# Attention and feed-forward on one core: the written-out order of the first 677 steps is replaced by another order of the same steps

## The chip, the core and the metric

The kernel runs on one core of a Trainium2 chip. The metric is the device time of one execution in microseconds (us). The instructions of the program are spread over five queues: TensorE (PE in the profile, its weight loads PEld), VectorE (DVE), ScalarE (ACT), GpSimd (POOL) and SyncE (SP, which issues most of the DMAs). Each queue runs its instructions in the order in which the program writes them, and waits on semaphores where one needs the result of another.

## What is computed

```python
scale = 1.0 / np.sqrt(q.shape[-1])                       # q, k, v: 8 x 12 x 448 x 64
scores = scale * np.matmul(q, k.transpose(0, 1, 3, 2)) - np.log(S)
attn = 1.0 / (1.0 + np.exp(-scores))                     # a sigmoid, no softmax
x = np.matmul(attn, v)                                   # to 3584 tokens x 768
h = x @ w_in                                             # 768 x 2048
g = np.where(h > 0.0, h, np.exp(np.minimum(h, 0.0)) - 1.0)
out = g @ w_out                                          # 2048 x 768
```

The eight batches have 448 tokens each. Both weights arrive as 64-bit floats. The kernel splits every operand of the feed-forward part into a high and a low fp16 part and adds three products.

## The kernel before

The work goes batch by batch: attention on pairs of heads, then the first layer (`moe1...`, x times w_in, 16 feature blocks f of 128), then the second layer (`moe2`, g times w_out). All queues are filled by hand (`manual_schedule`), so the order in which Python calls the steps is the order on every engine.

For the first part of the program that order is a table, `ORDER` (line 25), a text of 677 tokens. `first_stage` (line 1403) goes through it and calls one function for each token. A token's instructions go to the end of their engines' queues at that moment. So a token can only be moved against others of the same engine; across engines the semaphores decide. The table covers the attention of batches 0 and 1, the preparation of both weights, the first and second layer of batch 0, and ends where the first layer of batch 1 starts ("the second first layer": `next(h)` behind `first_stage`, line 1500). The tokens:

- `q k v i n` with a number load a pair's rows on SP. `T` turns queries and keys on TensorE, `Y` copies them, `Sn.t` makes scores, `Gn.t` is the sigmoid on ScalarE, `Vn.t` multiplies by the values on TensorE, `H` and `I` write the result's two parts, `M Q N` measure the values.
- `l A b B C D d E F` load and split one of eight units of w_in (`w_in_parts`, line 280). The 64-bit words lie in the tile `stage`.
- `x0` to `x15` are the products of batch 0's first layer, 18 matmuls each (`moe1_products`, line 890). `y` (ScalarE, line 907), `j` (VectorE), `z` (ScalarE, line 1390) and `w` (VectorE, line 1393) turn block f into g.
- `o0` to `o18` load w_out in 19 pieces (`w_out_parts`, line 436). For each piece, `a` (ScalarE, line 222) and `e` (ScalarE, line 230) take the words apart, `c` (VectorE, line 235) joins them, `g` adds their sizes on TensorE (line 244, tile `so`), `s` (VectorE, line 251) puts the sign back. When all pieces of a half have gone through `g`, `m0` or `m1` (`w_out_scale`, line 497) makes that half's scale, and only then `h` (ScalarE, line 475) and `p` (VectorE, line 481) write the fp16 parts. Pieces 0 to 7 are the first half, 8 to 18 the second.
- `X0` to `X95` are steps of three matmuls of batch 0's second layer (line 1115), sixteen to an output tile. X0 to X47 need the first half of w_out, X48 to X95 the second. `O0` to `O5` scale and store a tile.
- `K` is one piece of `make_sums` (line 422): VectorE and ScalarE write sums of blocks of w_in into the tile `room`, and the next `K` has GpSimd store them (line 420). `room` has three places for results. Later batches load these sums.

The raw words of a two-row piece of w_out are staged in the half of the tile `wo` that is not yet needed:

```python
SLOTS = 0, 4, 8, 12, 0, 4, 8, 12, 8, 12, 8, 12, 12      # by piece
w = wo[:, 1, SLOTS[k] : SLOTS[k] + 4]
```

So the load of piece 9 waits for `s7`, that of piece 11 for `s9`, that of piece 12 for `s11`: they share the place 12. Pieces 13 to 15 have a tile each, pieces 16 to 18 reuse them, so `o16` waits for `s13`.

Of the kernel before, what the change touches and what calls it, by code (L numbers as in the profile page):

```python
# [22 lines left out]

UNITS = 0, 4, 8
ORDER = """
n0 q0 q1 v0 i0 k0 k1 v1 l0 i1 T0 T1 Y0 q2 M0 Y1 S0.0 q3 S0.1 G0.0 l1 G0.1 Q0 S1.3 N0 v2
V0.0 G1.3 S0.2 b0 v3 S1.0 v13 V0.1 G0.2 k2 G1.0 S1.1 V0.2 A0 k3 V1.0 S1.2 G1.1 B0 G1.2
V1.1 C0 b1 l2 V1.2 D0 v12 V1.3 A1 M1 v4 T2 v5 H1 n1 H0 T3 I1 Y2 Q1 q5 I0 Y3 S2.0 S2.1
G2.0 N1 G2.1 S2.2 B1 V2.0 G2.2 q4 S3.3 d0 b2 S3.0 V2.1 G3.3 M2 l3 V2.2 E0 S3.1 k5 C1
G3.0 F0 Q2 k4 G3.1 S3.2 N2 V3.0 A2 V3.1 R0 G3.2 B2 b3 V3.2 V3.3 D1 T4 H2 d1 H3 T5 q6 Y4  # L30
C2 v7 I2 Y5 S4.0 l4 E1 S4.1 v6 I3 q7 R1 G4.0 k6 F1 G4.1 S5.3 V4.0 G5.3 D2 S4.2 A3 S5.0
d2 V4.1 G4.2 B3 l5 E2 S5.1 k7 V4.2 G5.0 M3 C3 G5.1 S5.2 V5.0 b4 D3 V5.1 F2 Q3 G5.2 T6 q8
Y6 V5.2 N3 A4 V5.3 d3 T7 H4 S6.0 q9 Y7 I4 v8 E3 S7.3 v9 B4 l6 G6.0 k8 F3 C4 G7.3 k9 S6.1
H5 V6.0 D4 G6.1 S6.2 I5 b5 V6.1 R2 S7.0 G6.2 d4 Rq G7.0 V6.2 S7.1 A5 Rr0 l7 S7.2 V7.0
G7.1 B5 G7.2 V7.1 T8 M4 V7.2 q10 C5 Y8 V7.3 b6 T9 Q4 S8.0 q11 H7 d5 H6 k10 Y9 D5 E4 I6
G8.0 S8.1 F4 v11 I7 v10 G8.1 V8.0 k11 S8.2 A6 N4 V8.1 G8.2 S9.0 B6 E5 V8.2 S9.1 M5 G9.0
C6 G9.1 S9.2 V9.0 b7 F5 V9.1 Q5 G9.2 T10 N5 q12 Y10 V9.2 d6 A7 S9.3 S10.0 D6 G9.3 B7
G10.0 S10.1 k12 V9.3 G10.1 r1 T11 H9 S10.2 H8 o13 I9 Y11 q13 C7 I8 G10.2 S11.3 r2 V10.0
V10.1 d7 D7 e13 S11.0 G11.3 k13 E6 V10.2 G11.0 F6 S11.1 S11.2 G11.1 V11.0 o14 G11.2 Wn
V11.1 E7 P12 V11.2 V11.3 x0 H10 o15 e14 H11 F7 I10 o0 x1 y0 Rr1 I11 e15 x2 y1 e0 o1 j1  # L40
a0 j0 z1 x3 c0 y2 z0 j2 w0 e1 o2 w1 z2 g0 x4 y3 s0 a1 w2 c1 j3 e2 o3 g1 x5 s1 y4 z3 j4
a2 w3 z4 c2 x6 y5 w4 o4 e3 j5 a3 z5 c3 g2 y6 w5 x7 s2 e4 o5 j6 a4 z6 c4 g3 x8 y7 w6 s3
j7 e5 o6 a5 g4 x9 s4 z7 y8 w7 c5 j8 a6 o7 g5 x10 s5 e6 y9 c6 z8 j9 w8 g6 z9 x11 s6 e7 w9
a7 o8 y10 c7 j10 g7 y11 x12 s7 z10 m0 e8 o9 w10 a8 x13 j11 h0 c8 y12 z11 p0 w11 e9 g8
x14 s8 a9 j12 o10 h1 c9 y13 z12 p1 g9 y14 x15 s9 h2 w12 p2 e10 o11 j13 a10 h3 c10 X0 X1
y15 p3 g10 z13 X2 s10 X3 h4 X4 j15 X5 e11 X6 a11 X7 p4 z15 c11 X8 h5 X9 w13 g11 s11 p5
o12 j14 X10 h6 X11 p6 z14 w14 X12 h7 X13 w15 p7 e12 X14 K a12 X15 X16 c12 X17 X18 O0 g12
X19 s12 X20 X21 a13 X22 a14 c13 X23 a15 X24 K c14 g13 c15 X25 s13 g14 g15 X26 s15 o16
X27 s14 o17 o18 X28 X29 X30 X31 X32 O1 X33 a16 X34 K e16 X35 X36 c16 X37 g16 X38 s16 X39
X40 e17 X41 a17 X42 K X43 c17 X44 g17 X45 s17 X46 X47 a18 O2 e18 c18 g18 m1 s18 h8 p8  # L50
X48 h9 X49 p9 X50 K h10 X51 p10 X52 h11 X53 p11 X54 h12 X55 p12 X56 h13 X57 h14 p13 p14
X58 K h15 X59 h16 p15 p16 X60 h17 X61 h18 p17 p18 X62 K X63 X64 K O3 X65 X66 K X67 X68 K
X69 X70 K X71 X72 K X73 X74 K X75 X76 K X77 X78 K X79 X80 K O4 X81 X82 K X83 X84 K X85
X86 K X87 X88 K X89 X90 K X91 X92 X93 X94 X95 O5
"""
TOP = 13
ATOP = 15
# [1587 lines left out]
```

## Time and profile before

| | |
|---|---|
| median of 3 runs | 1165.05 us (1164.81 to 1166.44) |
| the profiled execution | 1167.26 us, its span 1165.5 us |
| mean granted clock of TensorE | 0.993 |
| busy in the span: PE, DVE, ACT, POOL | 1120.0, 816.9, 769.0, 129.9 us |
| first matmul of batch 0's first layer (x0) | 118.60 us |
| first matmul of batch 1's first layer, behind the table | 239.80 us |

The profiled execution is one run of its own and 2.2 us above the median. The profile times start at the span's first instruction. A row of a timeline or of the chain of waits has the start and the length; what stands in square brackets is the time for which the engine was idle before, and what ended it. PEclk is the share of full speed that TensorE was granted: 1.00 is 2.4 GHz, 0.50 is 1.2 GHz.

### The profile page before, as it was taken

The numbers are of one execution on the slowest core, as the hardware profiler recorded it, in microseconds if no ns is written. First come the engines' busy times: TensorE is split into PE (matmuls) and PEld (weight loads), VectorE is DVE, ScalarE is ACT, GpSimd is POOL, SyncE is SP. The second block draws the span as 40 slices with busy tenths as digits, with TensorE's granted clock in tenths as the row PEclk, the third lists the DMA queues.
The fourth block names the chain that finished last, engine by engine and source line by source line (L and its number), as shares of the span: only waits on it lengthen the run. The fifth ranks groups of instructions, "written<-read, shape, count | busy, mean of one in ns | idle before, by whom it ended". The sixth has DMA issues, their size and how long they took to land.

```text
span 1165.5 us, 22286 instructions
## 1 busy us (share of the span) xinstructions
PE 1120.0 (96%) x8626; PEld 717.0 (62%) x8626; DVE 816.9 (70%) x1681; ACT 769.0 (66%) x1080; POOL 129.9 (11%) x351
## 2 busy tenths in 40 slices
PE   6898998899999999999999999999999999999998
PEld 2332454455544795559755796559755696559864
DVE  2888877778897668886686567886687567875500
ACT  5898786467865568686765568776776567775600
POOL 0000000333443000100010000100011010110000
PEclk9999999999999999999999999999999999999999
DMA  9873544234486295428644195527754195416100
GB/s 237 240 237 94 176 136 122 83 113 115 106 214 171 92 272 149 109 68 273 180 105 95 57 282 153 120 69 229 224 100 94 32 301 155 109 30 212 42 28 28
DMA packets 224666, 164.65 MB, mean 141 GB/s; under 512 B 170384, under 2 KB 189840, under 8 KB 224560
## 3 DMA queue, kind: packets, MB, share of 16 engines
q1 hardware_dynamic: 220400, 152.22, 47.6%
q0 software_dynamic: 4160, 11.01, 2.9%
q8 instruction: 67, 1.10, 0.4%
q14 instruction: 39, 0.32, 0.1%
HBM read 124.65 MB, written 22.02 MB: 126 GB/s over the span
## 4 chain that ended last, share of the span: by engine, by line
PE 69%; ACT 10%; DVE 9%; DMA 6%; issue 3%; SPq 2%; POOL 1%; ACTq 0%; DVEq 0%; POOLq 0%
PE po L1115 21%; PE X L1004 11%; PE ph L899 9%; PE psc L657 7%; PE pav L706 6%; PE po_r L1115 5%; PE Y L1004 3%; PE A L1004 3%; PE B L1004 3%; ACT sg L681 2%; DVE at L693 1%; DMA raw<-in_q_dram 1%; ACT g L1030 1%; DMA stage<-in_moe_w_in_dram 1%; PE pav L724 1%
## 5 line engine op out<-in xcount | busy, mean ns | idle before, releaser
L1115 PE MATMUL po<-wo,g 128*128 128x384 f16 x2304 | 393.5, 329 | 5.9 <-DVE wo L481 2.7
L1115 PEld LDWEIGHTS <-g 128*128 128x128 f16 x2688 | 258.5, 98 | 197.2 <-issue 30.1
L1004 PEld LDWEIGHTS <-wi 128*128 128x128 f16 x3024 | 288.3, 98 | 6.1 <-issue 4.4
L693 DVE SCALAR_TENSOR_TENSOR at<-sg,at 128x896 f16<-128x896 f32 x126 | 132.4, 1086 | 53.9 <-ACT at L692 53.9
L681 ACT ACTIVATE sg<-psc,bias,sc 128x896 f32<-128x896 f32 x108 | 114.8, 1091 | 43.0 <-PE psc L657 36.2
L1004 PE MATMUL X<-wi 128*128 128x224 f16 x1296 | 133.0, 259 | 1.5 <-DVE c L1051 1.5
L657 PE MATMUL psc<-qk 64*128 64x448 f16 (+2 forms) x960 | 109.6, 379 | 10.6 <-ACT sg L681 10.1
L692 ACT ACTIVATE at<-sg 128x896 f16<-128x896 f32 x126 | 113.4, 945 | 0.6
L899 PE MATMUL ph<-xh,wi 128*128 128x448 f16 x576 | 111.1, 352 | 0.0
L620 ACT ACTIVATE nat<-raw,sc 128x384 f16<-128x384 f32 (+1 forms) x108 | 51.2, 534 | 69.4 <-POOL sc L591 67.0
L899 PEld LDWEIGHTS <-wi 128*128 128x128 f16 x576 | 56.0, 98 | 53.1 <-issue 1.5
L591 POOL TENSOR_SCALAR sc<-sc 128x3 f32<-128x3 f32 x36 | 10.9, 303 | 606.3 <-DVE xs L551 432.0
L706 PE MATMUL pav<-at,vn 128*64 128x448 f16 x648 | 68.2, 355 | 0.0
L657 PEld LDWEIGHTS <-qk 64*128 64x128 f16 (+1 forms) x864 | 31.1, 97 | 57.0 <-issue 40.2
L1115 PE MATMUL po_r<-wo,g 128*128 128x384 f16 x384 | 64.3, 326 | 0.0
L1019 DVE SCALAR_TENSOR_TENSOR eb<-eb,c 128x896 f32<-128x896 f32 x24 | 26.2, 1090 | 49.6 <-ACT c L1016 49.6
L1125 DVE TENSOR_SCALAR o<-po,osc 128x384 f32<-128x384 f32 x48 | 29.3, 611 | 39.4 <-PE po L1115 38.6
L623 DVE SCALAR_TENSOR_TENSOR nat<-raw,sc,nat 128x384 f16<-128x384 f32 (+1 forms) x108 | 50.8, 524 | 7.0 <-ACT nat L620 7.0
L706 PEld LDWEIGHTS <-vn 128*64 128x64 f16 x648 | 33.6, 109 | 32.2 <-issue 13.0
L1004 PE MATMUL X<-xh,wi 128*128 128x224 f16 x432 | 45.4, 259 | 0.0
L1004 PE MATMUL Y<-xh,wi 128*128 128x224 f16 x432 | 45.3, 259 | 0.0
L1004 PE MATMUL B<-xh,wi 128*128 128x224 f16 x432 | 45.3, 259 | 0.0
(176 smaller groups left out, 1512.8 us busy)
## 6 DMA issues: line engine op xcount, KB each, us to landing
wi<-blend SPq DMA_DIRECT2D x168, 384.0 KB, 4.6
stage<-in_moe_w_in_dram SPq DMA_DIRECT2D x8, 1536.0 KB, 8.2
wo<-in_moe_w_out_dram SPq DMA_DIRECT2D x13, 768.0 KB, 4.5
raw<-in_q_dram SPq DMA_DIRECT2D x96, 96.0 KB, 3.3
raw<-in_k_dram SPq DMA_DIRECT2D x96, 96.0 KB, 3.1
out_dram<-o SPq DMA_DIRECT2D x48, 192.0 KB, 1.9
blend<-room POOLq DMA_DIRECT2D x38, 192.0 KB, 2.4
rv<-in_v_dram SPq DMA_DIRECT2D x36, 192.0 KB, 2.7
```

The source lines that it names most:

```text
L620: nc.scalar.mul(hi, src, s)
L623: nc.vector.scalar_tensor_tensor(lo, src, s, hi, op0=ALU.mult, op1=ALU.subtract)
L657: nc.tensor.matmul(psc[:, j, :S] if g < NC else psc[rows[x], j, :S], kk[rows[j], o], qq[rows[j], :S], start=(n == 0), stop=(n == n_parts - 1),
L681: nc.scalar.activation(sg, psc[:, :, :S], AF.Sigmoid, bias=bias, scale=scale)
L692: nc.scalar.mul(parts[0], sg, 2.0**ATOP)
L693: nc.vector.scalar_tensor_tensor(parts[1], sg, 2.0**ATOP, parts[0], op0=ALU.mult, op1=ALU.subtract)
L706: nc.tensor.matmul(pav[rows[j], :S], vv[i][:, j * NC + g if g < NC else 2 * NC + j], sg[k][:, j], start=(g == 0 and n == 0), stop=False,)
L899: nc.tensor.matmul(ph[:, :S], wi[:, NU - 1 - f // WF, wj, c, f % WF * P :][:, :P], hidden_of(b, c)[:, xj], start=(n == 0), stop=(n == 3 * ...
L1004: nc.tensor.matmul(to[:, j * HS : (j + 1) * HS], block[:, j, c, wj], rhs(k, c, xj), start=(k in (1, 5) and j == 0 and n == 0), stop=(j == ...
L1019: nc.vector.scalar_tensor_tensor(e, e, -1.0, src, op0=ALU.add, op1=ALU.min)
L1115: nc.tensor.matmul(po[:, :HM], lh(gj, f), wo[:, i, f, wj], start=(n == 0), stop=(n == 3 * NF - 1),)
L1125: nc.vector.tensor_scalar(o, po[:, :HM], sc, None, op0=ALU.mult)
```

## The change

Only the table is replaced. Both tables have the same 677 tokens, each once (`K` 21 times), in another sequence; on SP the loads stay in the same sequence up to the queries of pair 13; from there `o0` to `o3` come ahead of that pair's keys, and `o14` and `o15` later. Tiles get their buffers in the table's order, so buffer numbers change too. One line of the old table and one of the new:

```diff
-V11.1 E7 P12 V11.2 V11.3 x0 H10 o15 e14 H11 F7 I10 o0 x1 y0 Rr1 I11 e15 x2 y1 e0 o1 j1
+G11.0 V10.1 F6 V10.2 o13 S11.1 V11.0 E7 q13 F7 S11.2 G11.1 Wn G11.2 x0 o0 P12 y0 j0 x1
```

The first place is TensorE where batch 0's first layer starts. `psc` are scores, `pav` the products with the values (line 706; line 724 is the last one of two pairs), `ph` is the layer. Before:

```order
L657 MATMUL psc_5_989<-qk_5_922 128x448 x2
L706 MATMUL pav_5_994<-sg_5_975,vn_5_783 64x448 x2
L706 MATMUL pav_5_994<-sg_5_988,vn_5_783 64x448 x2
L706 MATMUL pav_5_994<-sg_5_992,vn_5_783 64x448 x2
L724 MATMUL pav_4_958<-sg_4_954,early 64x448 x2
L724 MATMUL pav_5_994<-sg_4_954,early 64x448 x2
L899 LDWEIGHTS wi
L899 MATMUL ph_0_1029<-xh_281,wi 128x448
```

With the change:

```order
L657 MATMUL psc_5_959<-qk_5_904 128x448 x2
L706 MATMUL pav_4_947<-sg_4_881,vn_4_856 64x448 x2
L706 MATMUL pav_4_947<-sg_4_933,vn_4_856 64x448 x2
L657 MATMUL psc_5_974<-qk_5_904 128x448 x2
L706 MATMUL pav_5_978<-sg_5_962,vn_5_805 64x448 x2
L657 MATMUL psc_5_987<-qk_5_904 128x448 x2
L899 LDWEIGHTS wi
L899 MATMUL ph_0_999<-xh_269,wi 128x448
```

Three products with the values (`V11.1`, `V11.2` of line 706 and `V11.3` of line 724) now stand behind x1, no longer ahead of the layer.

The second place is VectorE ahead of `m0`, the scale of w_out's first half (its first row is line 258). `ph_n` is block n of the layer, `to` or `wo` a piece of w_out. Before:

```order
L913 SCALAR_TENSOR_TENSOR e_8_1288<-e_8_1288,ph_9_1299 128x448
L1393 SCALAR_TENSOR_TENSOR g<-e_8_1288,msc_686,g 128x448
L251 SCALAR_TENSOR_TENSOR wo<-wo 128x768
L1393 SCALAR_TENSOR_TENSOR g<-e_8_1288,msc_686,g 128x448
L235 SCALAR_TENSOR_TENSOR to_14_1382<-to_14_1382,wo 128x768
L913 SCALAR_TENSOR_TENSOR e_10_1348<-e_10_1348,ph_10_1329 128x448
L251 SCALAR_TENSOR_TENSOR to_14_1382<-wo,to_14_1382 128x768
L258 TENSOR_REDUCE alw<-so_1145 128x1
```

With the change:

```order
L917 TENSOR_SCALAR e_4_1168<-e_4_1168 128x448
L918 SCALAR_TENSOR_TENSOR e_4_1168<-ph_5_1184,msc_730,e_4_1168 128x448
L917 TENSOR_SCALAR e_4_1168<-e_4_1168 128x448
L918 SCALAR_TENSOR_TENSOR e_4_1168<-ph_4_1149,msc_730,e_4_1168 128x448
L235 SCALAR_TENSOR_TENSOR wo<-wo 128x768
L251 SCALAR_TENSOR_TENSOR wo<-wo 128x768 x3
L235 SCALAR_TENSOR_TENSOR to_14_1272<-to_14_1272,wo 128x768
L1393 SCALAR_TENSOR_TENSOR g<-e_4_1168,msc_730,g 128x448
L258 TENSOR_REDUCE alw<-so_1110 128x1
```

The scale stood behind the layer's block 10 and now stands behind block 5: the first eight pieces of w_out come earlier against the layer, and the steps `w` (line 1393) and `j` of the layer come later.

The third place is VectorE ahead of `m1`, the scale of the second half. `so` are the last single pieces, line 1125 is `O` (which waits for the last matmul of a tile), line 352 is a part of `K`. Before:

```order
L235 SCALAR_TENSOR_TENSOR wo<-wo,so_13_1680 128x384
L251 SCALAR_TENSOR_TENSOR wo<-so_13_1680,wo 128x384
L352 TENSOR_TENSOR room<-room 128x3x128 x2
L235 SCALAR_TENSOR_TENSOR to_14_1747<-to_14_1747,so_14_1686 128x384
L251 SCALAR_TENSOR_TENSOR to_14_1747<-so_14_1686,to_14_1747 128x384
L1125 TENSOR_SCALAR o_2_0_1776<-po_2_0_1702,osc_1422 128x384
L235 SCALAR_TENSOR_TENSOR to_15_1774<-to_15_1774,so_15_1688 128x384
L258 TENSOR_REDUCE alw<-so_1460 128x1
```

With the change:

```order
L235 SCALAR_TENSOR_TENSOR wo<-wo,so_13_1651 128x384
L368 SCALAR_TENSOR_TENSOR room<-room,wt 128x3x128
L1125 TENSOR_SCALAR o_1_0_1719<-po_1_0_1628,osc_1286 128x384
L235 SCALAR_TENSOR_TENSOR to_14_1722<-to_14_1722,so_14_1667 128x384
L235 SCALAR_TENSOR_TENSOR to_15_1731<-to_15_1731,so_15_1694 128x384
L251 SCALAR_TENSOR_TENSOR wo<-so_13_1651,wo 128x384
L258 TENSOR_REDUCE alw<-so_1352 128x1
```

The last piece's `c` (line 235, `to_15`) no longer stands behind `O2`, which waits for X47; `O2` now comes behind `m1`. All six `K` that stand ahead of the last `p` now come between X18 and X28; four of six stood ahead of `m1` before, spread from X14 to X42.

On TensorE the twelve two-row sums come earlier against the layer: `g0` and `g1` stand ahead of x3 and `g7` ahead of x8, where they stood ahead of x4, x5 and x12; `g11` stands ahead of x15, where it stood ahead of X10.

## Rows read from the trace of the kernel before

**Rows 1.** Stretches: length, busy us of PE, PEld, DVE, ACT, POOL; clock; DMA.
```profile
81.50:118.60 37.10, 33.49 (x191) 12.13 (x189) 31.35 (x71) 31.29 (x31) 0.46 (x2) 1.00 0.43 115
118.60:176.50 57.90, 57.90 (x313) 30.01 (x310) 46.49 (x75) 44.40 (x68) 1.24 (x3) 1.00 0.51 152
176.50:212.80 36.30, 28.69 (x158) 15.58 (x158) 26.66 (x48) 19.88 (x38) 2.80 (x5) 0.95 0.32 107
212.80:223.80 11.00, 9.82 (x46) 4.92 (x46) 10.00 (x19) 9.70 (x18) 1.73 (x3) 0.84 0.09 36
223.80:240.00 16.20, 16.20 (x102) 9.69 (x100) 12.30 (x22) 6.19 (x11) 9.34 (x15) 1.00 0.50 159
240.00:295.00 55.00, 54.50 (x291) 28.04 (x289) 43.41 (x106) 37.28 (x77) 18.15 (x35) 1.00 0.40 107
185.67:189.09 3.42, 3.23 (x11) 1.24 (x9) 3.42 (x7) 2.20 (x5) 0.00 (x0) 0.50 0.72 222
212.98:216.39 3.41, 3.08 (x11) 1.44 (x10) 3.26 (x7) 2.94 (x7) 0.54 (x2) 0.50 0.00 0
```

**Rows 2.** TensorE's timeline: start, length, what, [idle before <-releaser].
```profile
192.71 0.50 PE L244 MATMUL so<-wo,ones 128*128 128x384 bf16 x2 [1.32 <-DVE wo L235]
...
210.31 0.33 PE L244 MATMUL so<-to,ones 128*128 128x384 bf16 x1 [1.17 <-DVE to L235]
212.77 0.32 PE L1115 MATMUL po<-wo,g 128*128 128x384 f16 x1 [2.14 <-ACT wo L475]
```

**Rows 3.** Chain of waits, 172 to 225 us: start, length, what.
```profile
184.53 4.43 DMA wo<-in_moe_w_out_dram
...
189.90 1.00 ACT room L386 x2
...
193.25 0.97 DVE wo L251
...
197.80 3.27 DMA so<-in_moe_w_out_dram
...
204.09 3.41 PE po L1115 x21
...
212.11 0.62 ACT wo L475
```

**Rows 4.** ScalarE's, then VectorE's timeline, 204 to 211 us.
```profile
204.86 0.55 ACT L230 ACTIVATE so<-so 128x384 uint32<-128x384 uint16 x1
...
209.17 0.62 DVE L1125 TENSOR_SCALAR o<-po,osc 128x384 f32<-128x384 f32 x1 [0.90 <-PE po L1115]
209.71 0.55 DVE L235 SCALAR_TENSOR_TENSOR to<-to,so 128x384 uint32<-128x384 uint32 x1
```

**Rows 5.** TensorE's timeline, 113 to 119 us.
```profile
114.33 1.02 PE L657 MATMUL psc<-qk 64*128 64x448 f32 x4 [1.32 <-ACT sg L681]
115.28 2.48 PE L706 MATMUL pav<-sg,vn 128*64 128x448 f32 x12
117.68 0.98 PE L724 MATMUL pav<-sg,early 64*64 64x448 f32 x8
```

**Rows 6.** Chain of waits, 110 to 172 us: one layer product.
```profile
132.73 3.40 PE ph L899 x18
```

**Rows 7.** TensorE's timeline: the first and eighth sum.
```profile
132.23 0.50 PE L244 MATMUL so<-wo,ones 128*128 128x384 bf16 x2
...
161.85 0.50 PE L244 MATMUL so<-to,ones 128*128 128x384 bf16 x2
```

**Rows 8.** Line 420, GpSimd's stores: ns min/median/max; landing of its DMAs.
```profile
L420 POOL DMA_DIRECT2D blend<-room x38: 540/542/776, 191.2 to 368.0; - x38
...
DMA to landing us min/median/max: 2.1/2.8/6.2
```

**Rows 9.** VectorE's, then TensorE's timeline, 241 to 244 us.
```profile
241.87 0.62 DVE L368 SCALAR_TENSOR_TENSOR room<-room,wt 128x384 f16<-128x384 f32 x1 [0.38 <-ACT room L364]
...
243.87 0.16 PE L191 MATMUL pb<-dg,ones 128*128 128x4 bf16 x1 [0.50 <-DVE dg L185]
```

More of the change, by code (lines that the diff above doesn't have):

```diff
@@ L25 @@
 ORDER = """
[L26 to L37, printed above, removed]
@@ L38 @@
-G10.0 S10.1 k12 V9.3 G10.1 r1 T11 H9 S10.2 H8 o13 I9 Y11 q13 C7 I8 G10.2 S11.3 r2 V10.0
-V10.1 d7 D7 e13 S11.0 G11.3 k13 E6 V10.2 G11.0 F6 S11.1 S11.2 G11.1 V11.0 o14 G11.2 Wn
-V11.1 E7 P12 V11.2 V11.3 x0 H10 o15 e14 H11 F7 I10 o0 x1 y0 Rr1 I11 e15 x2 y1 e0 o1 j1
-a0 j0 z1 x3 c0 y2 z0 j2 w0 e1 o2 w1 z2 g0 x4 y3 s0 a1 w2 c1 j3 e2 o3 g1 x5 s1 y4 z3 j4
-a2 w3 z4 c2 x6 y5 w4 o4 e3 j5 a3 z5 c3 g2 y6 w5 x7 s2 e4 o5 j6 a4 z6 c4 g3 x8 y7 w6 s3
-j7 e5 o6 a5 g4 x9 s4 z7 y8 w7 c5 j8 a6 o7 g5 x10 s5 e6 y9 c6 z8 j9 w8 g6 z9 x11 s6 e7 w9
@@ L44 @@
[L44 to L54, printed above, removed]
+n0 q0 q1 v0 i0 k0 T0 k1 T1 Y0 S0.0 v1 l0 Y1 i1 G0.0 S0.1 q2 q3 V0.0 S1.3 G0.1 S0.2 G1.3
+V0.1 l1 v2 S1.0 A0 G0.2 S1.1 V0.2 M0 v3 G1.0 b0 V1.0 Q0 S1.2 B0 G1.1 v13 G1.2 k2 k3 V1.1
@@ new lines @@
+N0 V1.2 A1 V1.3 l2 M1 b1 C0 v12 D0 H1 d0 T2 v4 T3 Q1 Y2 v5 S2.0 Y3 G2.0 n1 H0 B1 S2.1 N1
+q5 C1 q4 I0 S2.2 G2.1 D1 S3.3 M2 V2.0 E0 G2.2 F0 S3.0 V2.1 I1 G3.3 S3.1 V2.2 G3.0 V3.0
+b2 S3.2 G3.1 l3 d1 V3.1 A2 G3.2 Q2 k5 B2 V3.2 V3.3 E1 H2 k4 H3 T4 N2 q6 F1 I2 b3 T5 I3
+Y4 S4.0 Y5 v7 G4.0 S4.1 C2 S5.3 R0 G4.1 l4 R1 D2 S4.2 d2 V4.0 V4.1 A3 G5.3 G4.2 S5.0 B3
+E2 G5.0 v6 S5.1 V4.2 C3 M3 q7 G5.1 S5.2 k6 b4 V5.0 T6 F2 G5.2 D3 A4 Y6 l5 V5.1 V5.2 V5.3
+d3 Q3 B4 k7 E3 T7 S6.0 H4 Y7 C4 S7.3 G6.0 H5 S6.1 N3 I4 G7.3 q8 V6.0 D4 S6.2 I5 G6.1 R2
@@ new lines @@
+q9 S7.0 v8 v9 b5 V6.1 l6 F3 G6.2 G7.0 A5 k8 Rq S7.1 V6.2 d4 k9 B5 S7.2 V7.0 M4 G7.1 T8
+G7.2 C5 D5 b6 Rr0 T9 Y8 l7 V7.1 S8.0 V7.2 Y9 V7.3 E4 G8.0 S8.1 H7 F4 H6 S8.2 I6 q10 q11
+G8.1 Q4 V8.0 I7 G8.2 A6 k10 S9.0 G9.0 V8.1 S9.1 v11 d5 N4 B6 V8.2 E5 S9.2 V9.0 G9.1 G9.2
+b7 T10 Y10 C6 S9.3 G9.3 V9.1 v10 F5 S10.0 k11 A7 M5 V9.2 S10.1 G10.0 G10.1 d6 D6 Q5 V9.3
+B7 T11 N5 H9 H8 I8 Y11 q12 C7 S10.2 G10.2 D7 I9 k12 V10.0 d7 E6 S11.3 G11.3 S11.0 r1
+G11.0 V10.1 F6 V10.2 o13 S11.1 V11.0 E7 q13 F7 S11.2 G11.1 Wn G11.2 x0 o0 P12 y0 j0 x1
@@ new lines @@
+V11.1 y1 j1 V11.2 a0 o1 a1 o2 o3 e1 Rr1 V11.3 e0 x2 c1 H10 a2 a3 c0 k13 I10 e3 g0 g1 s0
+s1 e2 y2 x3 c2 g2 H11 c3 o4 z1 g3 o5 x4 y3 j2 s2 j3 z0 a4 z2 w1 e4 w0 e5 y4 c4 x5 a5 s3
+o6 I11 x6 c5 a6 y5 o7 g4 j5 j4 e6 g5 c6 z4 z3 z5 o14 g6 s4 x7 s6 s5 e7 a7 y6 c7 g7 w5 m0
+e14 e13 s7 w3 o8 w2 y7 x8 h0 a8 o9 o15 e8 j7 x9 y8 c8 j6 p0 g8 z7 w4 e9 a9 h1 s8 z6 j8
+y9 c9 p1 x10 h2 y10 j9 x11 o10 g9 w7 r2 w6 a10 p2 s9 e10 c10 y11 z9 o11 h3 j10 p3 j11 z8
+x12 g10 y12 x13 h4 e11 s10 p4 w9 j12 a11 w8 y13 x14 c11 h5 g11 j13 x15 X0 z10 y14 z13 X1
@@ new lines @@
+s11 z11 X2 X3 j14 o12 X4 z14 X5 X6 X7 p5 w13 h6 z12 w14 y15 w11 p6 a12 X8 w10 X9 w12 X10
+e12 j15 c12 g12 h7 X11 e15 z15 p7 X12 s12 w15 X13 X14 a14 X15 c14 a13 a15 X16 c13 X17
+c15 g13 g14 g15 O0 s13 X18 K o16 X19 X20 X21 s15 K o17 X22 s14 X23 K K X24 a16 K X25 o18
+e16 X26 c16 X27 K X28 X29 X30 X31 O1 a17 e17 X32 g16 c17 a18 X33 e18 c18 X34 g17 g18 X35
+s16 m1 s17 h8 X36 X37 s18 X38 X39 X40 X41 X42 p8 X43 h9 p9 h10 p10 X44 X45 h11 X46 X47
+p11 X48 h12 O2 p12 X49 X50 h13 X51 X52 X53 X54 X55 X56 X57 p13 h14 p14 h15 h16 X58 p15
@@ L55 @@
+p16 X59 h17 h18 X60 p17 X61 p18 K X62 X63 K X64 K K X65 X66 X67 O3 X68 X69 X70 K X71 X72
+X73 K X74 K X75 X76 X77 X78 X79 X80 X81 X82 K X83 X84 X85 X86 O4 K K X87 X88 X89 X90 X91
+X92 K X93 K X94 K X95 K O5 K
 """
```

## Prediction

> **What bounds the kernel now.** I read the busy times by stretch first, to find where TensorE, the busiest engine, is not kept busy. From 118.6 to 176.5 us it never stops (57.90 of 57.90), and so from 223.8 to 240.0 and, nearly, from 240 to 295 us (54.50 of 55.00) [rows 1]. Ahead of the first layer it is busy for 33.49 of 37.10 us while VectorE and ScalarE have 31.3 each: three engines at once near their end, little to win by order. The loss is between 176.5 and 212.8 us: 28.69 of 36.30, with VectorE and ScalarE at 26.66 and 19.88. There every engine waits for another.
>
> TensorE's timeline then names the waits: 1.32 us ahead of the sum of a piece of w_out, 1.17 us ahead of the last sum, 2.14 us for ScalarE's first `h` behind the scale `m1` [rows 2]. The chain of waits says what they hang on: the load of piece 12 at 184.53 us (4.43 us), its steps, then at 197.80 us the loads of the last pieces, and `h` at 212.11 us [rows 3]. So the stage ends by a chain of loads and short steps on three engines, and TensorE has nothing else to do meanwhile. The table decides how early that chain starts.
>
> **The sum now**, in four legs of the profiled execution, up to where the second layer's last matmul ends: x0 starts at 118.6; from there to the load of piece 12, 65.9 (184.53); to the first `h`, 27.6 (212.11); to the end, 27.9 (240.0).
>
> **Leg 1, up to x0: 118.6 becomes 116.0.** Ahead of x0 stand three products with the values that now stand behind it: two of the three in the 2.48 us of line 706, 1.65, and 0.98 of line 724, so 2.6 us [rows 5]. They are not saved, they move into the layer, where TensorE has no free time, so leg 2 pays for them. Leg 1 ends earlier by 2.6 if the rest goes as before. Two ends: nothing, if ScalarE sets the pace (TensorE waited 1.32 us for it just ahead [rows 5]); 3.9, if that wait goes too. I take 2.6: the waited-for sigmoid is still needed, and the products are not.
>
> **Leg 2, from x0 to the load of piece 12: 65.9 becomes 61.0.** The load waits for `s11`, and that for the sum `g11`. In the new table `g11` stands behind 15 products of the layer, eleven other two-row sums and the three products of leg 1. A layer product takes 3.40 us [rows 6]. A matmul of 384 columns takes 0.162 (21 in 3.41 [rows 3]), so a sum of two 0.33. That is 51.0 + 3.6 + 2.6 = 57.2; `g11` itself and `s` (as 0.97 [rows 3]) make 58.5. This holds if TensorE waits for no piece. It does not wait now in the layer, because the sums come late: the first at 132.23, 13.6 us behind x0, the eighth at 161.85, 43.2 behind [rows 7]. In the new table the eighth stands at 32 us by the same count. Each sum needs a load, three steps and its turn, so some will be late. Upper end: each of the twelve waits as the two seen above do, 1.2 us [rows 2], 14.4 in all; lower end none. I take 2.5, two waits, since two of the nineteen sums show such a wait now. What comes later for it, `w` and `j` of the layer, is covered: the second layer needs block f only at X0 plus f.
>
> **Leg 3, from that load to the first `h`: 27.6 becomes 25.3.** The loads (4.43 and 3.27) and the steps stay. ScalarE's last `e` ended at 205.4, but the `c` that follows ran at 209.71 behind `O2`, which stood from 209.17 behind a tile of TensorE's [rows 4]. With `O2` behind `m1` these 4.3 us go. Late next is TensorE itself, where the last sums stand behind X32 and X34. Against this, two more `K` fall into the leg, each about 1.0 on ScalarE (189.90 [rows 3]), on VectorE beside it: minus 4.3, plus 2.0. Bounds: 23.3 if the `K` hide, 29.6 if nothing is won and they don't.
>
> **Leg 4, from `h` to the end: 27.9 becomes 28.2.** Now TensorE stands with X48 to X95 left and waits for `p`. With the change X36 and its followers are left: 60 steps of three matmuls, 0.487 each, 29.2; two or so run during `m1`, which leaves 28.2. The `h` and `p` pairs need 11.7 us (212.1 to 223.8) and hide behind the first 24 of these steps. So the engine that waited becomes the bound: the end moves by as much as `h` does, no more.
>
> **The sum:** 116.0 + 61.0 + 25.3 + 28.2 = 230.5 against 240.0, 9.5 us sooner. Behind it batch 1's first layer waits for the chain of `K`: in the run before, its scale matmul came at 243.87 after a wait of 0.50 for VectorE, whose last `K` ran at 241.87 [rows 9]. The fifteen `K` behind the last `p` are the same in both tables and start with it, so this end moves too. The layer that follows is bound by TensorE [rows 1], and nothing behind it has changed but buffer numbers, so the gain should last to the end. The profiled execution took 1167.26 us, so 1157.8; the median of the three runs is 2.2 lower, 1165.05, so **1155.5 us**.
>
> **Half clock.** Twice in the slow stretch TensorE was granted 0.50 for 3.4 us [rows 1], after the waits above. It cost the chain nothing: in the first a load was under way, in the second `p` set the pace. Fewer waits should take both away, at no price and no gain; one new stretch inside the first layer, where TensorE is the bound, costs half of 3.4, 1.7.
>
> **Rivals.**
>
> A, slower: the sums hold the layer up. TensorE runs its queue in order, so a sum that waits stops every layer product behind it, and the layer was the one stretch without a wait. With 1.2 us at each of the twelve, leg 2 is 72.9 and the end 242.4: 1167.5. It decides from a wait of 1.0 us a sum, 12.0 in all. For it: the eighth sum comes 11 us sooner, and its place in the staging tile must be emptied and loaded twice by then. Against it: VectorE and ScalarE have 11 and 13 us free in that stretch [rows 1]. The Trainium skill says the same of the order (PSUM — Partial Sum Buffer, section Engine vs sequencer instructions): matmuls start and complete in program order. The idle time at the sums in rows 2 agrees.
>
> B, a smaller gain: x0 does not come sooner (the lower end of leg 1) and a half-clock stretch falls into the layer: 9.5 - 2.6 - 1.7 = 5.2, so 1160.
>
> C, `room`: six `K` in ten steps of X, with three places. A store lands 2.1 to 2.8 us after its issue [rows 8], and a place is wanted again three results later; at two waits of 2.8 in ScalarE's queue ahead of the last `a`, leg 3 is 30.9 and the gain 3.9: 1161. The issue itself is short, 0.54 us in the median and 0.78 at most [rows 8], beside a busy VectorE. The Trainium skill would make more of it: SBUF — State Buffer, section SBUF: two separate sides, says that a DMA issued from GpSimd's queue can be held up while VectorE holds their shared port, 620 ns alone growing to 3100. By that figure five more early stores could add up to 12 us, an estimate from that page. The 38 stores of rows 8 show nothing like it, so I keep the row's price.
>
> D, the change does nothing: what is won in legs 2 and 3 is paid back as waits in the layer. 1163 to 1167.
>
> **How the numbers follow.** A measurement of this kernel can tell about 0.2%, 2.3 us. Chances: the forecast within its bounds 0.64, A 0.12, B 0.12, C 0.06, D 0.06. The first, B and most of C are faster by over 0.2%: 0.80. D and the edge of A and C are the same: 0.09. Slower, 0.11, is A. The low end of the range has leg 1 at 114.7 and leg 2 at 58.5: 226.7, 13.3 us, 1151.7, and a little below, 1150.5, for `K` that hide in leg 3. The high end takes in B, C and half of D: 1165.0. Left out is A and the little beyond the low end.
>
> **What would show it.** Right: x0 near 116; piece 12 loaded near 177 and not 184.5; the first `h` near 202; TensorE busy for nearly all of the time between 176 and the end of the table near 230.5; no granted clock of 0.50 there. Leg 2 is wrong if TensorE's timeline shows waits of a microsecond ahead of the sums between the layer's products; leg 3 if ScalarE waits for a store's landing; leg 4 if TensorE still waits ahead of X48. The forecast as a whole is wrong if the second first layer starts later than 236.

## The result and the profile after

The changed kernel takes **1149.49 us** in the median of four runs (1147.72 to 1151.70), against 1165.00 for the kernel before on the same chip: a ratio of **0.9865, 95% interval 0.9845 to 0.9886**, 15.5 us less. On two other chips the same pair gave 0.9853 (0.9832 to 0.9875) and 0.9855 (0.9824 to 0.9886). The forecast was 1155.5 with a range of 1150.5 to 1165.0: the sign holds, and so does the mechanism of legs 2 to 4; leg 1 does not. The gain came out 6 us larger than forecast, and the range ended 1 us above the result. The profiled execution took 1147.72 us with a span of 1145.9.

The four legs of the prediction, read from the profiles:

| leg, us | before | forecast | the change | the change, two more profiles |
|---|---|---|---|---|
| 1, start to x0 | 118.6 | 116.0 | 110.6 | 109.1, 113.3 |
| 2, x0 to the load of piece 12 | 65.9 | 61.0 | 59.4 | 59.4, 59.7 |
| 3, that load to the first `h` behind `m1` | 27.6 | 25.3 | 24.0 | 24.0, 23.8 |
| 4, that `h` to the end of X95 | 27.9 | 28.2 | 28.3 | 28.3, 28.3 |
| end of the table | 240.0 | 230.5 | 222.3 | 220.8, 225.1 |

Legs 2 to 4 are the same in all three profiles within 0.3 us, and leg 1 is not. The stretches of the change that answer to [rows 1]: length, busy us of PE, PEld, DVE, ACT, POOL, then the granted clock and the DMA.

```profile
81.50:110.62 29.12, 28.91 (x156) 9.64 (x157) 26.72 (x57) 27.28 (x27) 0.00 (x0) 1.00 0.35 92
110.62:172.24 61.62, 61.41 (x331) 31.09 (x330) 54.83 (x98) 50.10 (x79) 3.38 (x5) 1.00 0.56 173
172.24:194.08 21.84, 20.68 (x125) 12.01 (x124) 20.25 (x40) 15.06 (x29) 2.70 (x6) 1.00 0.40 139
194.08:222.34 28.26, 28.26 (x175) 17.02 (x174) 22.93 (x40) 15.84 (x28) 11.29 (x18) 1.00 0.33 105
222.34:277.34 55.00, 55.00 (x298) 28.26 (x295) 43.81 (x106) 37.66 (x78) 18.14 (x35) 1.00 0.40 107
```

From x0 on TensorE is now idle for 0.21 + 1.16 us in all up to the end of the table, and the 0.50 us ahead of batch 1's scale [rows 9] is gone (55.00 of 55.00). Ahead of x0 the stretches can be compared only from the same token on: T8 came at 81.55 us before and comes at 77.41 now, so the first row above leaves out 4 us behind T8. From T8 on it is:

```profile
77.41:110.62 33.21, 31.59 (x178) 11.85 (x177) 29.74 (x66) 30.10 (x30) 0.00 (x0) 1.00 0.43 120
```

From T8 to x0 TensorE was idle for 3.61 us [rows 1] and now is for 1.62, of which 1.41 is one wait for keys (in the two more profiles 0.21 and 1.96 us, the second with 1.76 for keys). That leg is where the forecast missed. The waits of TensorE up to x0, from 20 us, first before, then with the change (us in total, times, longest):

```profile
PE psc L657 <- ACT sg L681: 3.4, 3, 1.3
PE pt L1283 <- DMA raw<-in_k_dram: 2.4, 2, 1.3
PE pav L706 <- ACT sg L681: 2.0, 2, 1.4
PE si L244 <- DVE stage L235: 1.3, 1, 1.3
PE psc L657 <- ACT early L1299: 0.8, 2, 0.6
```

```profile
PE psc L657 <- ACT early L1299: 2.0, 2, 1.8
PE pt L1283 <- DMA raw<-in_k_dram: 1.4, 1, 1.4
PE si L244 <- DVE stage L235: 0.8, 1, 0.8
PE psc L657 <- ACT sg L681: 0.7, 1, 0.7
PE pav L706 <- ACT sg L681: 0.4, 2, 0.3
```

The waits for ScalarE's sigmoids (`sg`) fall from 5.4 to 1.1 us, those for its copies (`early`) grow from 0.8 to 2.0. Around x0 the timeline of TensorE with the change (start, length, what) shows the three products of leg 1 now between x1 and x2, and the first sums 12.9 us behind x0, with no idle time ahead of them:

```profile
110.62 6.98 PE L899 MATMUL ph<-xh,wi 128*128 128x448 f16 x36
117.54 1.72 PE L706 MATMUL pav<-sg,vn 128*64 128x448 f32 x8
119.19 0.98 PE L724 MATMUL pav<-sg,early 64*64 64x448 f32 x8
120.11 3.58 PE L899 MATMUL ph<-xh,wi 128*128 128x448 f16 x18
123.52 0.84 PE L244 MATMUL so<-wo,ones 128*128 128x384 bf16 x4
```

In the stretch that was slow, what is left of TensorE's waits in [rows 2] is 1.15 us, ahead of the last three sums:

```profile
189.91 0.33 PE L244 MATMUL so<-wo,ones 128*128 128x384 bf16 x1 [0.42 <-DVE wo L235]
...
191.43 0.33 PE L244 MATMUL so<-to,ones 128*128 128x384 bf16 x1 [0.22 <-DVE to L235]
192.28 0.33 PE L244 MATMUL so<-to,ones 128*128 128x384 bf16 x1 [0.51 <-DVE to L235]
```

The load of piece 12 is issued at 170.06 us and not at 184.53, `h` starts at 194.08 and not at 212.11 (SyncE's, then ScalarE's timeline). Neither half-clock stretch of [rows 1] is there.

```profile
170.06 0.37 SPq L449 DMA_DIRECT2D wo<-in_moe_w_out_dram  x1
...
194.08 1.12 ACT L475 ACTIVATE wo<-wo,swo 128x384 f16<-128x384 f32 x2 [2.45 <-DVE swo L501]
```

### The profile page after: what moved, and what is told of

Read it like the earlier page. It is cut to its first block, busy times and chain, and to the rows that moved or that the text cites. A ratio compares the mean times of both kernels' runs of the same rounds, so it can differ in the third digit from the quotient of the medians.

```text
span 1145.9 us, 22290 instructions
## 1 busy us (share of the span) xinstructions
PE 1113.4 (97%) x8626; PEld 715.9 (62%) x8626; DVE 815.5 (71%) x1681; ACT 768.1 (67%) x1080; POOL 131.7 (11%) x351
## 4 chain that ended last, share of the span: by engine, by line
PE 71%; ACT 13%; DVE 8%; DMA 5%; issue 3%; SPq 1%; POOL 0%; ACTq 0%; DVEq 0%; POOLq 0%
PE po L1115 23%; PE X L1004 11%; PE ph L899 7%; PE psc L657 7%; PE pav L706 6%; PE po_r L1115 5%; PE Y L1004 3%; PE A L1004 3%; ACT sg L681 3%; PE B L1004 2%; ACT g L1030 1%; DMA raw<-in_q_dram 1%; PE pav L724 1%; DVE at L693 1%; DMA blend<-room 1%
## 5 line engine op out<-in xcount | busy, mean ns | idle before, releaser
L1115 PE MATMUL po<-wo,g 128*128 128x384 f16 x2304 | 387.8, 327 | 1.3 <-DVE g L1036 1.3
```

Of the source, the lines that this page charges most:

```text
L1115: nc.tensor.matmul(po[:, :HM], lh(gj, f), wo[:, i, f, wj], start=(n == 0), stop=(n == 3 * NF - 1),)
```

## The experiments

All kernels differ from the change in the table alone, and hold each token once. "Old up to T, then new" means: the old table up to the token T, then what is left in the new table's order. Ratios are to the kernel before on the same chip.

### The part ahead of x0, and the rest

```diff
-ORDER: new
+h1: old up to T4, then new        # old-to-T4
+h2: old up to T8, then new        # old-to-T8
+h3: old up to x0, then new        # old head
+h4: new up to x0, then old        # new head
```

> The table of the change, but with the old sequence up to the token T4 (47 us). Two theories of the 8.0 us by which x0 starts sooner (118.6 to 110.6) where I forecast 2.6. Theory P (pace): the old sequence loses the time piecemeal, where TensorE waits for ScalarE's sigmoids; up to T4 the two tables stand level (47.36 and 47.15), so nothing is lost here: x0 at 110.6 to 111.0, time 1149.5 to 1150. Theory C (clock): the stretch at half clock at 32 to 35.5 us, which only the old sequence has, is 1.7 us lost on the path; it comes back with the old start: x0 at 112.3, time 1151.2.

> The old sequence up to the token T8 (81.5 us before, 77.4 in the change), the change's behind it. Theory P: the 4.1 us lost between T4 and T8 are lost again, no more: x0 at 114.7, time 1153.6. Theory C: only the 1.7 us of the half clock: 1151.2. A third, S (slack): ScalarE's work that the old sequence has behind is made good by TensorE's idle time between T8 and x0: 1149.5.

> The old sequence up to x0, the change's behind it. Theory K (kept): the legs add up, and what x0 is late is late at the end: x0 at 118.6, second first layer's last matmul at 230.3, time 1149.5 + 8.0 = 1157.5, which is 2.0 above my forecast because the half-clock stretches and the layer's sums cost nothing. Rival L (later): the early sums of the change need loads that only the early x0 leaves time for; then TensorE waits in the layer and the time is 1160 or more. Rival M (made good): the layer's free time takes it back, 1152 or less.

> The change's sequence up to x0, the old one behind it. Theory K: 8.0 of the 15.5 us are won: x0 at 110.6, 1157. Rival M: the old rest waits for chains of loads and steps whose pace x0 doesn't set, so part of the 8.0 is lost in waits: 1159 to 1163.

Measured: the old sequence up to T4 0.9860 (0.9843 to 0.9877), up to T8 0.9854 (0.9835 to 0.9874), both the change's time; the old head whole 0.9916 (0.9899 to 0.9932); the new head with the old rest 0.9977 (0.9965 to 0.9989). x0 is at 113.0, 110.2, 117.1 and 112.5 us, the last step X95 starts at 224.4, 221.0, 227.6 and 233.0 (the change 221.7, before 239.3). The old start did not bring back the half-clock stretch at 32 us, and by the time the first run is P and not C. (Its x0 fits neither theory; this profile has a half-clock stretch of its own, at 51 to 55 us, and a wait of 1.47 us for keys.) So the new sequence up to T8 is worth nothing by itself (S): with the old one there T8 comes 1.8 us later than in the change, and x0 does not. What leg 1 wins needs the sequence behind T8. With the old head x0 is 6.5 us later than in the change and X95 5.9: what x0 loses is lost at the end too (K, with a smaller sum than I gave, since x0 came at 117.1 and not at 118.6). The new head with the old rest has the time that M gave, but not by its mechanism: from x0 to the end of the table it takes 121.1 us, where the two profiles of before (the second is below) take 121.4 and 121.2, so nothing is lost behind x0. The head by itself wins less than 8.0; its profile of 112.5 is one of an execution 1.5 us below its median. 2.7 us for the new head alone and 9.8 for the new rest alone make 12.5 and not 15.5 to 17: some 3 to 5 us come only with both. In these two tables, unlike the change, V11.1 to V11.3 stand ahead of x0.

### The three products, and a second profile of before

```diff
-S11.2 G11.1 Wn G11.2 x0 o0 P12 y0 j0 x1 V11.1 y1 j1 V11.2 a0 ... Rr1 V11.3 e0
+S11.2 G11.1 Wn G11.2 V11.1 V11.2 V11.3 x0 o0 P12 y0 j0 x1 y1 j1 a0 ... Rr1 e0
```

> The kernel before once more, for a second profile. Theory R: the half-clock stretch at 32.07 to 35.49 us is this one execution's, x0 then comes at 116.5 to 117.5 without it, and 1.5 of the 8.0 us of leg 1 are no merit of the change. Theory T: the stretch comes with the old table, x0 at 118.0 to 119.0 again.

> The change again, beside the next two on their chip: x0 at 109 to 111, X0 at 170.5 to 172.5, 0.985 to 0.987 of before.

> The change with the three products V11.1, V11.2 and V11.3 ahead of x0 again, as before. By the step of the prediction in question (they are not saved, they move into the layer): x0 2.4 to 2.6 us later than the change, X0 and the time as the change within 0.5 us. Rival G (won): the products fill no gap ahead of x0, but ahead of the layer they wait for the last sigmoid G11.2: x0 3.5 us or more later, X0 1 us or more later, the time too.

The kernel before has x0 at 117.43 in its second profile, with the clock at 1.00 from 28 to 36 us: 1.2 of the 8.0 us belong to that one execution (R). TensorE's busy time up to x0 differs by only 0.4 of this (97.70 and 97.33 us), the rest is idle time, so the half-clock stretch alone does not make it. The change has x0 at 113.31 in the third profile; TensorE was at the lower clock there just after a wait for keys:

```profile
81.00:84.42 3.42, 3.42 (x17) 2.55 (x17) 1.51 (x10) 1.53 (x3) 0.00 (x0) 0.57 0.95 336
```

With the products ahead of x0 again the ratio is 0.9887 (0.9862 to 0.9912) beside 0.9855 for the change on that chip, 1151.5 against 1146.9 us. x0 comes at 113.85, 3.2 us later than in the change's first profile, whose time up to there is otherwise alike (S11.2 at 109.84 and 109.67), and X0 at 174.74, 2.5 later. So the products are won and not moved (G, though at x0 it gave 3.5 or more), but the place of the gain is not the one I had named: TensorE's timeline of this kernel, then VectorE's, show it behind x2.

```profile
112.03 0.97 PE L706 MATMUL pav<-sg,vn 128*64 128x448 f32 x4 [0.27 <-ACT sg L681]
...
113.85 10.39 PE L899 MATMUL ph<-xh,wi 128*128 128x448 f16 x54
126.40 0.84 PE L244 MATMUL so<-wo,ones 128*128 128x384 bf16 x4 [2.16 <-DVE xh L779]
...
123.92 1.83 DVE L235 SCALAR_TENSOR_TENSOR wo<-wo 128x768 uint32<-128x768 uint32 x2 [0.73 <-ACT wo L230]
125.66 0.68 DVE L779 SCALAR_TENSOR_TENSOR xh<-pav,sc,xh 128x448 f16<-128x448 f32 x1
```

The wait ahead of g0 ends with VectorE's `I10` (line 779), which reads pair 10's products out of the bank that the first sums are written to. It stands right behind the `c` of the first pieces (line 235), and these wait for ScalarE, which takes the pieces apart only behind the layer's first two `y`. The products fill just that time: without them there TensorE waits 2.16 us ahead of g0.

### One late step of VectorE

```diff
-q13 C7 I8 G10.2 S11.3 r2 V10.0 V10.1 d7 D7 e13
+q13 C7 D7 I8 G10.2 S11.3 r2 V10.0 V10.1 d7 e13
```

> The table of before with one token moved: D7, VectorE's scale of the last unit of w_in, from behind r2, V10 and d7 to right behind C7, whose sum it needs. In the profile of before ScalarE stands idle for 2.10 us ahead of E6 for it, and TensorE 1.32 us ahead of S11.2 for the sigmoid behind E6. Theory D (one late step of VectorE): E6 starts with no wait, x0 1.3 to 2.1 us sooner against T8 (37.0 us from T8 to x0 become 35.0 to 35.7), time 1 to 2 us lower. Rival S (sigmoids): TensorE waits at its sums of scores wherever ScalarE is full, and the wait only moves to another place ahead of x0: T8 to x0 stays at 36.5 to 37.0 and the time does not change.

> The change itself beside the others of this call, on their chip: 14 to 17 us under the kernel before. Its profile shows which half-clock stretches of TensorE come with the table and which fall anew in each execution: by theory R (random) none of the stretches is at the same place as in the first profile of the change, but x0 is again at 110 to 111 us; by theory T (table) the one at 325 to 335 us is there again.

This edit is made in the old table. ScalarE stood there as the first row shows, and no longer does; but TensorE, in the second row, now waits ahead of V10.0, whose bank VectorE frees with the step that D7 has passed (I8).

```profile
111.80 1.57 ACT L323 ACTIVATE wi<-stage,swi 128x1536 f16<-128x1536 f32 x1 [2.10 <-DVE swi L305]
```

```profile
107.69 1.72 PE L706 MATMUL pav<-sg,vn 128*64 128x448 f32 x8 [0.91 <-DVE xh L779]
```

From T8 to x0 it takes 36.4 us and not 37.0, and the ratio is 0.9999 (0.9986 to 1.0013): the wait moved (S). The change, run beside it, was at 0.9853, and its stretch at half clock came at 325 to 335 us again (T); in the third profile, above, it came at 360 to 365, so the table doesn't fix the place.

### The layer's sequence, and the tail's

```diff
-ORDER: new
+e2: new up to x0, old up to X0, then new      # old layer
+e3: new up to X0, then old                    # old tail
```

> The change with the old sequence inside batch 0's first layer (behind x0 up to X0), so with the sums g0 to g11 late again; head and tail are the change's. Theory K (chain): the load of piece 12 comes 66 us behind x0 again (before 65.9, the change 59.4), at 176.5, the rest as in the change: 24.0 to the first h, 28.3 to the end: 228.8 and not 222.3, time 6.5 above the change. Rival B (TensorE bound): the second layer's first steps fill the wait and the end moves by 3 us or less.

> The change up to X0, the old sequence behind it (O2 ahead of c18, the K late, the last sums' places between X as before). Theory K: the load of piece 12 near 170, from there 27.6 to the first h instead of 24.0, then 27.9 to the end: 226, time 3.5 above the change. Rival B: with piece 12 loaded 14 us sooner against X0 than before, nothing is late any more in the old tail, the end is bound by TensorE as in the change, and the time is the change's within 1 us. Rival W: the old places of the sums between the X steps make TensorE wait as before, 5 us or more.

Both cost more than theory K gave, and the second is in W's range: 0.9929 (0.9906 to 0.9953) and 0.9964 (0.9952 to 0.9976), 9 and 13 us above the change. In the first, g10 and g11 came to stand directly ahead of X0 with their pieces not ready, and TensorE did what rival A says, this time in front of the second layer's steps:

```profile
172.65 0.50 PE L244 MATMUL so<-wo,ones 128*128 128x384 bf16 x2 [1.11 <-DVE wo L235]
176.91 0.80 PE L244 MATMUL so<-wo,ones 128*128 128x384 bf16 x2 [3.76 <-DVE wo L235]
```

In the second the sum g11 is early (172.30), but the old tail has its sign step `s11` behind steps of the layer that wait for ScalarE. VectorE's timeline:

```profile
177.41 0.62 DVE L913 SCALAR_TENSOR_TENSOR e<-e,ph 128x448 f32<-128x448 f32 x1 [1.72 <-ACT ph L909]
177.99 0.69 DVE L1393 SCALAR_TENSOR_TENSOR g<-e,msc,g 128x448 f16<-128x448 f32 x1
178.59 0.95 DVE L251 SCALAR_TENSOR_TENSOR wo<-wo 128x768 uint32<-128x768 uint32 x1
```

So the load goes out at 179.62, and the early sum has bought nothing. From X0 to the end of X95 TensorE is idle for 6.8 us, 8.8 before: W's size, but with the load late as well, so the sums' places are not shown to be its cause. Over all profiles the last step X95 starts 51.0 to 51.7 us behind that load with the new tail, in eleven kernels, and 54.6 to 54.8 with the old one, in four, whatever stands ahead. The new tail alone is worth 3.1 us.

### That load alone

```diff
-X2 X3 ... p5 w13 h6 z12 w14 y15 w11 p6 a12     (s11 ahead of X2, o12 behind X3)
+X2 X3 ... p5 w13 h6 z12 w14 y15 w11 p6 s11 o12 a12
```

> The change with two tokens moved: s11, VectorE's sign step of piece 11, and the load o12 that waits for it, from ahead of X3 to behind p6. It tests leg 2 alone, with TensorE's sequence untouched. Theory K (the load of piece 12 sets the end: in the seven profiles with the change's tail the last step X95 starts 51.6 us behind it): s11 at 175, o12 at 176 and not 170, X95 at 227.6 and not 221.7, the time 5.5 to 6 us above the change. Rival B (the end is TensorE's, and the load had slack): the time 2 us or less above the change.

The ratio is 0.9914 (0.9882 to 0.9945), 1153.8 us against 1146.9: theory K, with 6.9 us where it gave 5.5 to 6. The load goes out at 175.51, X95 starts at 227.0, and TensorE, whose queue was not touched, stands ahead of g12:

```profile
182.78 0.80 PE L244 MATMUL so<-wo,ones 128*128 128x384 bf16 x2 [5.33 <-DVE wo L235]
```

The load was moved to a later place only; an earlier one was not tried.

### One engine's sequence alone

The 310 tokens that the change has ahead of x0 (the old table has 309 of them there), in the old sequence on some engines and in the new on others; where the two are mixed, a token stands as early as what it needs allows. Behind them the new table.

```diff
-old head                                  # h3
+f0: the 310 tokens old on every engine
+f1: S V T C Q (TensorE) new, others old
+f2: G A b E H Y (ScalarE) new, others old
+f3: TensorE and ScalarE new, others old
```

> The old sequence up to x0 on every engine, but with only the work in it that the change has there (V11.1 to V11.3, r2, P12, e13, o14 and k13 behind x0); the change's behind it. It parts the 8.0 us of leg 1 into work moved and waits. Theory M (moved, not saved): x0 2.6 us sooner than with the old head whole (117.1 to 114.5), X0 where it was (178.1), time as with the old head, 1154 or 0.992 of before. Rival G (won): TensorE has waits in the layer that the three products fill, or the wait ahead of S11.2 goes too: X0 at 175.5 or less, 1151.5 or less.

> As the kernel with all engines old ahead of x0, but TensorE's own sequence there is the change's; ScalarE, VectorE and SyncE keep the old one. Theory T (TensorE's sequence makes the 4 us of waits for sigmoids go): x0 at 110 to 111, time as the change, 0.985 of before. Theory A (ScalarE's sequence does): x0 at 114 to 115 as with all old, 0.991. Theory J (only together): 113 to 114, or later than all old, since S and V then stand against the sequence of the sigmoids.

> The same with ScalarE's sequence new and the others old. Theory A: x0 at 110 to 111, 0.985. Theory T: 114 to 115, 0.991. Theory J: 113 to 114 or later than all old.

> TensorE's and ScalarE's sequence new, VectorE's and SyncE's old. Theories T, A and J: x0 at 110 to 111, 0.985. Theory V (VectorE's sequence counts: D7 behind r2, I8 and d7 keeps ScalarE waiting, and a bank of V is freed late): x0 at 112.5 or later, 0.988 or more.

All old: 0.9888 (0.9869 to 0.9906) beside 0.9916 for the old head whole, x0 at 112.4 beside 117.1 and X0 at 175.6 beside 178.1. Of both 1.3 us stand already at T8, up to where the two tables are alike; what is left, 3.4 at x0 and 1.2 at X0, is again G: part of the work put behind x0 is won. The other three: 1.0085, 1.0056 and 1.0108, x0 at 135.4, 136.0 and 139.2 us. Mixed sequences cost 23 to 27 us ahead of x0, far past J. In the first, TensorE's new places for C and Q and VectorE's old places for B and N do not fit (PE's waits, then DVE's, from 20 to 135 us; line 244 is C, line 195 is N behind Q):

```profile
PE si L244 <- DVE stage L235: 10.5, 3, 4.0
```

```profile
DVE al L195 <- PE pb L191: 24.8, 5, 10.7
```

Not all of this is waiting: from 20 us to x0 the granted clock is 0.88, 0.89 and 0.90 in these three and 1.00 with all old, and TensorE is busy there for 95.8, 96.2 and 91.7 us and not for 84.7. So 7 to 11 us of the 23 to 27 are stretches at half clock, and the rest is idle time. These runs cannot part the gain among the engines. They show that the three sequences have to fit each other. The sequence of VectorE alone was not tried.

## Why the prediction was wrong

**Leg 1 failed**, at "I take 2.6" with its bounds of 0 and 3.9, and at its ground, "three engines at once near their end, little to win by order". x0 came 8.0 us sooner. 1.2 of it is the execution (x0 is at 117.43 in the second profile of before). The three products moved give 3.2 with the wait ahead of them. The remaining 3.6, from that second profile to the table with the products back, are TensorE's waits, since it is busy for 97.33 us up to x0 in both: those for sigmoids fell from 6.6 to 1.4, and those for copies (0.7 to 1.9) and for keys (1.0 to 1.7) gave a part back. Each of these terms rests on one profile a side, and x0 of the change alone varies by 4 us, so they are rough. By the ratios, which don't hang on single executions, the new head with the products still ahead of x0 is worth 2.7 us and their move 3.7 (0.9887 against 0.9855): 6.4 where the leg had 2.6. The rows for the waits were there: 3.61 us of idle time in the stretch of [rows 1] that I read as full, 3.38 of it for sigmoids, and none of that is left behind T8. I took only the last of these waits, 1.32 us [rows 5], into the bound. So the sum was too high even at its low ends: 114.7, 58.5 and 23.3 for legs 1 to 3 give 1149.7 us.

One token alone won nothing, and the new sequence on one or two engines alone lost 23 to 27 us. That the gain needs the places of all engines at once is likely from this and not shown; which places make it stays open.

**"They are not saved, they move into the layer, where TensorE has no free time"** was wrong as well. The layer had no free time with its sums late. With them early it has 2.2 us ahead of g0, and the products lie there: leg 2 is 58.7 us with the products ahead of x0 and 59.4 with them inside it, so it pays 0.7 for them and not 2.6. The tables with head or rest alone have the products ahead of x0, and lack the 3.7 us that their move wins: 2.7, 9.8 and 3.7 make 16.2, the 15.5 to 17 of the change.

**Leg 2** was right in mechanism and in size within 1.6 us: the load came 59.4 us behind x0. The 2.5 us for two waits at the sums was the term too many; the layer has 0.21 us of waits, so the lower bound of 58.5 was nearly met. That a later load of piece 12 makes the end later is shown by moving it alone.

**Leg 3**, 24.0 where 25.3 was forecast: the first of the last loads lands 16.8 us behind the issue of piece 12's load (16.5 before), and from there to `h` it takes 7.2 us and not 11.0. So the 4.3 us of `O2` are gone and 0.5 came back, where I had put 2.0 for the two `K` more; `O2` and the `K` were not tried one by one. **Leg 4** was right to 0.1: TensorE is busy for all of it.

**The rivals.** A did not occur in the change, and occurs in the table with the old layer. C's wait is there, in all three profiles (3.09, 3.09 and 3.08 us): ScalarE stands ahead of a step of `K` until a store has landed. It lies on the chain that ends last, and it is the sign that the prediction gave for leg 3 being wrong. Yet it cost little: the load that ScalarE takes up next had landed only at 186.84 us, and TensorE loses by the whole chain the 1.15 us above. (In four other tables with this tail the same wait, 2.9 to 3.0 us, is put down to VectorE's line 352, so the landing is not the only thing that it hangs on.) My price for a landing, 2.1 to 2.8 us, was the least and the median of [rows 8], whose longest is 6.2. The three stores issued between 182 and 185 us landed after 4.7, 4.3 and 4.7 us, where the first three before took 2.1 to 2.4. The hold-up of GpSimd's stores that I weighed from the Trainium skill (SBUF — State Buffer, section SBUF: two separate sides) does not show in their issues, which take 540 ns in the median and 776 at most, nearly as in [rows 8]. Whether it has a part in the longer landings no run here shows; loads of the last pieces ran at the same time.

```profile
187.27 0.61 ACT L364 ACTIVATE room<-room,wt 128x384 f16<-128x384 f32 x1 [3.09 <-DMA blend<-room]
```

**Half clock.** Both stretches of the slow part went, as forecast. Behind the table the change's profile has one and that of before two; from the end of the table on it is 923.6 us long against 925.5. The profiled executions lie 2.2 above and 1.8 below their medians, so their difference, 19.5 us, overstates the gain.

No version was found that beats the change: old up to T8 with the new rest is its equal, and of TensorE's idle time between x0 and the end of the table 1.4 us are left.

## What to carry to other kernels

Where three engines are each 84 to 90% busy, count the waits of the one that bounds the end, wait by wait from the first to the last: here they held what the new order won ahead of x0 beside the moved products, and the busy shares hid it. Work moved behind a milestone is not paid back if the place it goes to has a wait of its own, and a change made elsewhere can open that wait. A step brought forward on one engine delays the steps that it passes, and the wait can move to whoever needs those, as it did from D7 to I8.

## What was not expected

The same table starts x0 between 109.1 and 113.3 us: in one profile TensorE waits 1.41 us for keys ahead of a row that starts at 79.48, in another not at all, and in a third it waits 1.76 us and is at the lower clock right behind. The row of the first profile:

```profile
79.48 0.52 PE L1283 MATMUL pt<-ident,raw 128*128 128x128 f32 x3 [1.41 <-DMA raw<-in_k_dram]
```

Where one head's time varies by 4 us from one execution to the next, a single profile can't part terms of one or two.
